# Turned query features for more row pairs, with their key sums weighed by GpSimd: a linear-attention and gMLP kernel on one Trainium2 core

## The chip, the cores and the metric

The kernel runs on one core of one Trainium2 chip. The metric is the device time of one execution in microseconds (us). Several executions are timed and the median is taken; one further execution is recorded by the hardware profiler.

The engines are called by their short names: PE (TensorE, matrix products and transposes by a matmul with the identity), DVE (VectorE), ACT (ScalarE), POOL (GpSimd), SP (SyncE, which here only issues DMA transfers). Each has an instruction queue of its own and works through it in order.

## The reference

Two blocks read the same `x` of 2048 rows and 512 columns, in float32, and their results are added to it: `x + A(layernorm(x)) + B(layernorm(x))`.

```python
# A: linear attention, 32 heads of 16, Hedgehog features (32 per head)
pq = einsum("bhsd,hdf->bhsf", q, w_phi); pk = the same of k
phi_q = concat([softmax(pq), softmax(-pq)]); phi_k = the same of pk
kv  = einsum("bhsf,bhsd->bhfd", phi_k, v)
z   = einsum("bhsf->bhf", phi_k)                    # key sums
num = einsum("bhqf,bhfd->bhqd", phi_q, kv)
den = einsum("bhqf,bhf->bhq", phi_q, z) + 1e-6
o   = num / den;  A = o @ wo
# B: gMLP with 688 gated columns
u, v = split(gelu(xn @ w_in));  v = layernorm(v)
v = w_sp @ v + b_sp;            B = (u * v) @ w_out
```

## The kernel before, in words

The 2048 rows are 16 row tiles of 128 (`NT`), taken as 8 pairs. A tile's query features are 1024 values a row (`NF`). Products in float32 are made of three matmuls of high and low parts (`mm3`, lines L56 to L58).

The work goes through four stages. To about 205 us: projections, key features, `kv` and the key sums. The softmax exponentials of the queries (`e`) go to a DRAM tensor `e_d`. To about 290 us: the inputs of the gate. To 489 us: the spatial product with `w_sp` (tile name `g`), in 32 chunks, four for each pair of row blocks. After a pair's last chunk, `gate` multiplies by `u` and turns the result on DVE in blocks of 32x32, and DMAs store it to `u_d` and `ur_d` in a layout from which it can be loaded already transposed. From 489 us on, the last stage goes over the pairs; this is the loop `for i in range(0, NT, 2)` of the kernel. For each pair PE does: the projection of the gated values of tile i (`project_u`, `pout<-wu,...`), the attention of the pair (`attend`, `po<-f,kvT`), `project_u` of tile i+1, and the output projection of both tiles (`project_o`), whose result is added to `out` in DRAM by an accumulating DMA from POOL's queue (`out<-xr`, L1022).

`attend` needs the features transposed: features on the partitions. There are two ways to that.

- *Transposed on PE.* `attend_T` makes sixteen transposes for a pair (`ptq`, L972 or L974), and ACT copies the results out of PSUM (`f<-ptq`, L976).
- *Turned.* `turn_q` turns the tile on DVE in 32x32 blocks (STREAM_TRANSPOSE `qtmp<-et`, L559), four DMAs store it to the DRAM tensor `q_d` (L562), and one loads it transposed (`f<-q_d`, L564). PE has nothing to do. Tiles from `TQ` = 10 on (pairs 5 to 7) go this way.

Ahead of either, `q_fin` finishes a tile's features, all on DVE: the product of the exponentials with the key sums `zb` (L545, `qtmp<-et,zb`), a sum over each half head (L546), four small steps that make the factor `w` (L547 to L550), and the product of the exponentials with it (L552). `load_q` loads a tile's exponentials from `e_d` to a tile `et` by SP's queue. Tiles 4 to 9 are then copied from `et` into a buffer of the pair, `er`, by a DMA of POOL's queue (L940), from which PE transposes them; tiles 2 and 3 are transposed from `et` itself; tiles 0 and 1 have been finished much earlier and are loaded as `eq` by `first_q`.

`ahead(i)` runs after a tile's output projection and does the work for later ones: `features(i+3)`, the load of the exponentials of tile i+5, and of the gated values of tile i+4. The order of instructions on each engine comes from a scheduler, which follows the order of the code and the points set by `tc.issue_after`. `GATE_LAST` names the iteration in which the last pair's gate is made.

Of the kernel before, what the change touches and what calls it, by code (L numbers as in the profile page):

```python
# [10 lines left out]
F32 = mybir.dt.float32  # L11
F32R = mybir.dt.float32r
AF = mybir.ActivationFunctionType
ALU = mybir.AluOpType
# [26 lines left out]
def mixer(ctx: ExitStack, tc: tile.TileContext, x, x_t, wv, wqkT, phi_bd, wo, w_in, wst, b_r, w_out, out):  # L41
    nc = tc.nc
    pe, act, dve, pool, sp = nc.tensor, nc.scalar, nc.vector, nc.gpsimd, nc.sync
# [27 lines left out]
    def xz_tile(n, dt, name):  # L71
        return xz.tile([P, SL], dt, tag="xz", name=name)[:, :n]
# [3 lines left out]
    e_d = dram.tile([NT, P, NF + 2 * H], F32, name="e_d")  # L76
# [5 lines left out]
    q_d = dram.tile([NT, P, NF], F32, name="q_d")  # L82
# [16 lines left out]
    def heads(ap):  # L99
        return ap.rearrange("p (h d) -> p h d", d=DH)  # L100
# [76 lines left out]
    with ExitStack() as p0:  # L177
        res = p0.enter_context(left("p0res", 1))
        wk = p0.enter_context(left("p0wk", 2))
# [253 lines left out]
        p = ps.tile([P, D], F32, tag="mm", name="proj")  # L433
# [7 lines left out]
        p = ps.tile([P, D], F32, tag="mm", name="proj")  # L441
# [18 lines left out]
        p = ps.tile([P, D], F32, tag="mm", name="proj")  # L460
# [77 lines left out]
        sp.dma_start(et[:, :NF + 2 * H], e_d[s])  # L538
        return et

    def q_fin(et, tmp, zb):

        e, r, t, w = et[:, :NF], *(et[:, NF + k * 2 * H:NF + (k + 1) * 2 * H] for k in range(3))
        den = et[:, NF + 6 * H:QW]
        dve.tensor_tensor(tmp, e, zb, op=ALU.mult)  # L545
# [6 lines left out]
        return e, dve.tensor_tensor(heads(e), heads(e), bc(w, 2 * H), op=ALU.mult).ins  # L552

    TQ = 10

    def turn_q(s, dst, e, f, eng):

        NC8 = NF // P
        dve.transpose(dst.rearrange("p (m c t) -> p m c t", c=NC8, t=BL), e.rearrange("p (c m j) -> p m c j", c=NC8, j=BL))  # L559
        w = NC8 * BL  # L560
        for b in range(P // BL):
            eng.dma_start(q_d[s, :, b * w:(b + 1) * w].rearrange("(m j) w -> j m w", j=BL),  # L562
                          dst[b * BL:(b + 1) * BL].rearrange("p (m w) -> p m w", w=w))
        eng.dma_start(f[:, s % 2], q_d[s])  # L564

    QC = 4
    NQ = NT // QC
# [151 lines left out]
    for s in range(NT):  # L719
        p = zproj((kv_ps_p, zc, zbp, za)[s % 4], s, w2, (0, 1) if s % 2 == 0 else (1, 0))  # L720
# [7 lines left out]
        for k, q in p:  # L728
            ins = act.activation(z[:, k], q, AF.Gelu_apprx_tanh, scale=r_x[:, s:s + 1]).ins
# [30 lines left out]
    gt = mid.enter_context(right("gt", 1))  # L760
# [64 lines left out]
    def slot(name, dt=F32):  # L825
        return xz_tile(2 * FH, dt, name)
# [27 lines left out]

    lasts, wu = [None] * 9, []

    def first_q(s):
        e = slot("eq", F32R)[:, :NF]
        sp.dma_start(e.bitcast(F32), e_d[s, :, :NF])
        return e  # L860
# [11 lines left out]
    g, es, ets, ft, ep = {}, {}, {}, {}, {}  # L872
    for n in range(NC):
        i = SEQ[n][0]
        if n % NQ == 1 and i < NP - 1:
            z = load_z1(i)
        products(n, g)
        if n % NQ == NQ - 1 and i < NP - 1:
            c = gt.tile([P, 2, FU], F32, tag="c", name="c")
            cq = c[:, :, :FH].rearrange("p k (j f) -> p k j f", j=2)  # L880
            cb = drain(i, g, cq)
            g = {}
        if n + 3 < NC:
            raw[n + 3] = load_a(n + 3)
        if n + 2 < NC:
            A[n + 2] = prep_a(n + 2, raw.pop(n + 2))
        if n % NQ == NQ - 1 and i < NP - 1:
            turn = gate(i, cb, z, c, z, prep_a.last)
            if i < NP - 2:
                turn()  # L890
        if n == NC - 4:
            stage_w()
        if n == NC - 3:
            zs = slot("zb", F32R)
            zb, ident_r = zs[:, :NF].bitcast(F32), zs[:, NF:NF + P]
            round_h(act, ident_r, ident)
            sp.dma_start(zb, zb_d)
            uT = [first_gate(0)]
            ets[2] = load_q(2, slot("et"))
            es[2], last = q_fin(ets.pop(2), slot("qtmp")[:, :NF], zb)  # L900
        if n == NC - 2:
            es[0], es[1] = first_q(0), first_q(1)
            t = xz_tile((KF + 1) * P, F32R, "u1")
            us = {1: load_u(1, t[:, :KF * P].bitcast(F32), t[:2 * REM, KF * P:(KF + 1) * P])}
    cb = drain(NP - 1, g, slot("c").rearrange("p (k j f) -> p k j f", k=2, j=2))
# [6 lines left out]
    gt = p2.enter_context(right("gl", 1))  # L912
    cw = ctx.enter_context(left("cw", 1))
    wk = ctx.enter_context(left("cwk", 2))
    fin = []

    def fetch_u(i):
        return load_u(i, cw.tile([P, KF * P], F32, tag="u", bufs=4, name="u"),
                      cw.tile([2 * REM, P], F32R, tag="rt", bufs=6, name="rt"))

    def er_pair(name):
        return cw.tile([P, 2, NF], F32R, tag="er", bufs=3, name=name)

    def features(s):
        with tc.issue_after(fin[-1]):
            tmp = slot("qtmp")[:, :NF]
            es[s], ins = q_fin(ets.pop(s), tmp, zb)
        fin.append(ins)
        if s == 3:
            return  # L930
        if s >= TQ:
            if s % 2 == 0:
                ft[s] = er_pair("f").bitcast(F32)
            turn_q(s, tmp, es.pop(s), ft[s - s % 2], pool)
            return
        e = es[s]
        if s % 2 == 0:
            ep[s] = er_pair("er")
        es[s] = ep[s - s % 2][:, s % 2]
        lasts[6] = pool.dma_start(es[s].bitcast(F32), e).ins  # L940
# [18 lines left out]

    def attend_T(s):  # L960

        if s in ft:
            t = ft[s].rearrange("p k (b c t) -> p (k b) c t", c=NF // P, t=BL)
            return [t[:, :, 2 * g:2 * g + 2].rearrange("p b c t -> p c b t") for g in range(NG)]
        fs = []
        for g in range(NG):
            pt = pst.tile([P, 2, 2, P], F32, tag="tr", name="ptq")
            for a in range(2):
                for k in range(2):
                    src = group(es[s + k], 2 * g + a)  # L970
                    if src.dtype == F32:
                        pe.transpose(pt[:, a, k], src, ident)  # L972
                    else:
                        pe.transpose(pt[:, a, k].bitcast(F32R), src, ident_r)  # L974
            f = wk.tile([P, 2, 2 * P], F32, tag="f", bufs=NG + 1, name="f")
            lasts[5] = act.activation(f, pt.rearrange("p a k b -> p a (k b)"), AF.Copy).ins  # L976
            fs.append(f)
        return fs
# [47 lines left out]
                dve.tensor_tensor(xr[:, cs], q, xr[:, cs], op=ALU.add)  # L1026
                sp.dma_start(out[rows, cs], xr[:, cs])

    GATE_LAST = 8

    fT = attend_T(0)
    wk.tile([P, D], F32, tag="xr", bufs=3, name="xr")
    wk.tile([P, 10 * QP], F32, tag="gap", name="gap")
    wk.tile([P, NG, 2 * P], F32R, tag="oTh", name="oT")
    with tc.issue_after(lasts[5]), tc.issue_after(lasts[1]), tc.issue_after(fin[-1]):
        for c in range(ND):
            rows = [(m * QP, (m + 1) * QP) for m in range(c // 2 * 8 + c % 2, (c // 2 + 1) * 8, 2)]
            load_w(wo, rows, wo_h[:, c], wo_l[:, c], cw.tile([P, D], F32, tag="wof", bufs=4, name="wof"))
# [5 lines left out]

    def ahead(i):

        if 3 < i + 3 < NT:
            features(i + 3)
        if i + 5 < NT:
            ets[i + 5] = load_q(i + 5, slot("et"))  # L1050
        if i + 4 < NT:
            us[i + 4] = fetch_u(i + 4)

    p, nxt = {}, dict(enumerate(uT))
    for i in range(0, NT, 2):
# [60 lines left out]
```

## Time and profile before

| what | us |
|---|---|
| median of 3 runs | 618.63 (618.36 to 619.22) |
| the profiled execution's own time | 618.89 |
| its span, first to last instruction | 617.0 |
| PE busy | 610.3 (99%) |
| DVE busy | 517.6 (84%) |
| ACT busy | 269.6 (44%) |
| POOL busy | 128.8 (21%) |

The span starts with the first instruction and ends with the last; the execution's own time has 1.9 us more around it. Busy shares are means over stages of different kinds. In the last stage, the place of this change, what counts is the order in which things come due there: PE is dense, and the rows that follow in the prediction tell what comes just in time for it. In profile rows "idle before <-" names what ended an engine's wait, and a transfer's time is given from its issue to its landing.

### The profile page before, as it was taken

The page shows a single profiled execution, that of the slowest core. Times are in us where ns is not written, and L with a number is a line of the kernel's source. Part 1 is how long each engine was busy: PE and PEld are TensorE (multiplying, and loading weights), DVE is VectorE, ACT ScalarE, POOL GpSimd, SP SyncE. Part 2 cuts the span into 40 slices and gives each one's busy share as a digit, 9 for nine tenths or more (in the row PEclk, how much of TensorE's full clock was granted, in tenths as well). Part 3 has the DMA queues.
Part 4 walks back from the last instruction along what each step waited for, and adds up shares of the span by engine and source line. Part 5 has one row for each costly group of instructions (what it writes and reads, how often), then busy time and mean ns, then how long its engine had stood idle before and what let it go on. Part 6 is the DMA issues. An engine that isn't in the chain of part 4 may idle for free.

```text
span 617.0 us, 11407 instructions
## 1 busy us (share of the span) xinstructions
PE 610.3 (99%) x4318; PEld 557.1 (90%) x4318; DVE 517.6 (84%) x925; ACT 269.6 (44%) x424; POOL 128.8 (21%) x226
## 2 busy tenths in 40 slices
PE   8999999999999999999999999999999999999997
PEld 6888888888889999999999999999999987777775
DVE  5999999999978498989899898797979889999711
ACT  5653334323523467876444444344436343333221
POOL 4123232232110015442000000000000132234330
PEclk9999999999999999999999999999999999999999
DMA  8557876666446768001463744636355798987873
GB/s 308 196 136 168 227 176 173 156 163 171 125 141 163 263 218 289 2 1 35 149 144 122 198 101 148 155 95 186 97 164 181 222 364 287 303 239 210 221 161 65
DMA packets 55534, 106.81 MB, mean 173 GB/s; under 512 B 12136, under 2 KB 22248, under 8 KB 55240
## 3 DMA queue, kind: packets, MB, share of 16 engines
q1 hardware_dynamic: 40424, 60.77, 32.4%
q0 software_dynamic: 12752, 39.69, 25.2%
q10 hardware_dynamic: 2304, 5.64, 2.4%
q8 instruction: 34, 0.56, 0.4%
q14 instruction: 20, 0.16, 0.1%
HBM read 64.76 MB, written 33.71 MB: 160 GB/s over the span
## 4 chain that ended last, share of the span: by engine, by line
PE 95%; DMA 3%; DVE 0%; SPq 0%; ACT 0%; issue 0%; DVEq 0%; ACTq 0%
PE g L58 11%; PE g L57 11%; PE g L56 11%; PE proj L57 7%; PE proj L56 7%; PE proj L58 7%; PE zps L56 6%; PE zps L57 6%; PE zps L58 6%; PE pout L56 6%; PE pout L58 5%; PE pout L57 5%; PE po L989 1%; PE kvps L355 1%; PE pout L1003 1%; DMA wst__2228<-in_w_in 1%
## 5 line engine op out<-in xcount | busy, mean ns | idle before, releaser
L57 PE MATMUL g<-B,A 128*128 128x344 f32 x448 | 143.4, 320 | 0.0
L56 PE MATMUL g<-B,A 128*128 128x344 f32 x448 | 142.9, 319 | 0.0
L58 PE MATMUL g<-B,A 128*128 128x344 f32 x448 | 140.4, 321 | 0.1
L56 PEld LDWEIGHTS g<-B,A 128*128 128x128 f32 x448 | 84.3, 188 | 0.0
L57 PEld LDWEIGHTS g<-B,A 128*128 128x128 f32 x448 | 84.2, 188 | 0.0
L58 PEld LDWEIGHTS g<-B,A 128*128 128x128 f32 x448 | 83.6, 188 | 0.4 <-DVE A L52 0.4
L48 ACT ACTIVATE A<-S 128x512 fp32r<-128x512 f32 x64 | 40.1, 629 | 59.4 <-PE g L58 28.4
L52 DVE TENSOR_TENSOR A<-S,A 128x512 fp32r<-128x512 f32 x64 | 43.7, 686 | 11.2 <-ACT A L48 11.0
L48 ACT ACTIVATE A<-wf 128x512 fp32r<-128x512 f32 (+1 forms) x64 | 33.4, 523 | 44.5 <-PE g L58 28.1
L56 PE MATMUL proj<-wqk_h,xT 128*128 128x512 f32 x128 | 50.1, 391 | 0.0
L58 PE MATMUL proj<-wqk_h,xT 128*128 128x512 f32 x128 | 49.8, 389 | 0.0
L57 PE MATMUL proj<-wqk_l,xT 128*128 128x512 f32 x128 | 49.8, 389 | 0.0
L123 ACT ACTIVATE e<-e,r_x 128x1024 f32<-128x1024 f32 x26 | 29.7, 1148 | 42.3 <-DVE e L122 41.3
L768 POOL DMA_DIRECT2D z1t<-z_d x16 | 8.7, 546 | 162.5 <-DMA wf<-in_wst 127.2
L56 PE MATMUL zps<-w_0h,xT 128*128 128x344 f32 x128 | 41.0, 320 | 0.1
L57 PE MATMUL zps<-w_1l,xT 128*128 128x344 f32 x128 | 40.8, 319 | 0.0
L57 PE MATMUL zps<-w_0l,xT 128*128 128x344 f32 x128 | 40.8, 319 | 0.0
L58 PE MATMUL zps<-w_0h,xT 128*128 128x344 f32 x128 | 40.8, 319 | 0.0
L56 PE MATMUL zps<-w_1h,xT 128*128 128x344 f32 x128 | 40.7, 318 | 0.0
L58 PE MATMUL zps<-w_1h,xT 128*128 128x344 f32 x128 | 40.6, 319 | 0.0
L52 DVE TENSOR_TENSOR A<-wf,A 128x512 fp32r<-128x512 f32 (+1 forms) x64 | 35.3, 555 | 3.5 <-ACT A L48 3.3
L126 DVE TENSOR_REDUCE sm<-e 128x64 f32<-128x1024 f32 x26 | 31.1, 1201 | 2.5 <-ACT e L123 2.4
(224 smaller groups left out, 1435.9 us busy)
## 6 DMA issues: line engine op xcount, KB each, us to landing
wf<-in_wst SPq DMA_DIRECT2D x64, 256.0 KB, 3.2
e_d<-e POOLq DMA_DIRECT2D x16, 544.0 KB, 4.6
et<-e_d SPq DMA_DIRECT2D x16, 544.0 KB, 6.3
z_d<-z1f ACTq DMA_DIRECT2D x16, 344.0 KB, 2.9
z1t<-z_d POOLq DMA_DIRECT2D x16, 344.0 KB, 4.5
zacc<-e POOLq DMA_DIRECT2D x10, 512.0 KB, 4.9
u<-u_d SPq DMA_DIRECT2D x15, 320.0 KB, 5.9
xt<-in_x SPq DMA_DIRECT2D x16, 256.0 KB, 3.7
```

The lines of the kernel that those rows point to most:

```text
L48: return act.activation(h, src, AF.Copy).ins
L52: return (eng or dve).tensor_tensor(l, src, h.bitcast(F32), op=ALU.subtract).ins
L56: pe.matmul(dst, ah, bh, start=start, stop=False)
L57: pe.matmul(dst, ah, bl, start=False, stop=False)
L58: return pe.matmul(dst, al, bh, start=False, stop=stop).ins
L123: softmax_pair.last = less, act.activation(e, e, AF.Exp, scale=scale).ins
L126: dve.tensor_reduce(sm, heads(e), axis=AX.X, op=ALU.add)
L355: i = pe.matmul(kv_acc[k:k + QP, m // 4], vs[:, m * QP:(m + 1) * QP], e[:, m * HP:(m + 1) * HP], start=first and m < 4 and len(ready) == n ...
L768: pool.dma_start(t[:, k, :FH], z1_d[2 * i + k])
L989: lasts[3] = pe.matmul(po[r][c * QP:(c + 1) * QP, k], kvT[rows, m // 2, cols], fs[m // 4][rows, m // 2 % 2], start=True, stop=True).ins
L1003: lasts[2] = pe.matmul(p, rt, w, start=False, stop=i == NT - 1 and k == 1).ins
```

## The change

It has six parts.

1. `TQ` goes from 10 to 6: tiles 6 to 9 (pairs 3 and 4) are turned instead of transposed on PE.
2. Pair 0 is turned too, already in the stage before: after the gates of i = 2 and i = 4, tile 0's and tile 1's features are loaded from `e_d`, turned by DVE and stored to `q_d`. Four loads `f<-q_d` of 256 KB take the place of the two loads of `eq`.
3. For tiles 4 to 15 the product with the key sums is made by POOL, in a new function `weigh`, called from `ahead`. `q_fin` leaves it out there.
4. The stores to `q_d` and the loads of `f` go by SP's queue instead of POOL's (those of pair 0's early turn are stored by POOL's).
5. `GATE_LAST` goes from 8 to 6, one pair sooner.
6. The point after which the output weights are loaded is another (`lasts[0]` for `lasts[5]`), since pair 0 has no copies `f` any more.

Pairs 1 and 2 are still transposed on PE, and only tiles 4 and 5 still have an `er` copy.

```diff
-    def q_fin(et, tmp, zb):
+    def q_fin(et, tmp, zb, weighed=False):
...
-        dve.tensor_tensor(tmp, e, zb, op=ALU.mult)
+        if not weighed:
+            dve.tensor_tensor(tmp, e, zb, op=ALU.mult)
...
-    TQ = 10
+    TQ = 6
...
-        eng.dma_start(f[:, s % 2], q_d[s])
...
+            if i in (2, 4):
+                s = i // 2 - 1
+                e, t = (gt.tile([P, 2, FU], F32, tag=tag, name=name).rearrange("p k f -> p (k f)")[:, :NF]
+                        for tag, name in (("c", "c"), ("z1", "z1t")))
+                pool.dma_start(e, e_d[s, :, :NF])
+                turn_q(s, t, e, pool)
...
-            es[0], es[1] = first_q(0), first_q(1)
+            fq = [slot("f")[:, :NF].rearrange("p (k b c t) -> p k b c t", k=2, c=NB // 2, t=BL) for h in range(2)]
+            for k in range(2):
+                for h in range(2):
+                    sp.dma_start(fq[h][:, k], q_d[k].rearrange("p (b h w) -> h p b w", h=2, w=QB // 2)[h])
...
+    def weigh(s):
+        weighed[s] = slot("qtmp")[:, :NF]
+        pool.tensor_tensor(weighed[s], ets[s][:, :NF], zb, op=ALU.mult)
...
-            tmp = slot("qtmp")[:, :NF]
-            es[s], ins = q_fin(ets.pop(s), tmp, zb)
+            tmp = weighed.pop(s, None)
+            if s > 3:
+                es[s], ins = q_fin(ets.pop(s), tmp, zb, True)
+            else:
+                tmp = slot("qtmp")[:, :NF]
+                es[s], ins = q_fin(ets.pop(s), tmp, zb)
...
-            turn_q(s, tmp, es.pop(s), ft[s - s % 2], pool)
+            turn_q(s, tmp, es.pop(s), sp)
...
-    GATE_LAST = 8
+    GATE_LAST = 6
...
-    with tc.issue_after(lasts[5]), tc.issue_after(lasts[1]), tc.issue_after(fin[-1]):
+    with tc.issue_after(lasts[0]), tc.issue_after(lasts[1]), tc.issue_after(fin[-1]):
...
+        if i + 4 < NT:
+            weigh(i + 4)
         if 3 < i + 3 < NT:
             features(i + 3)
...
+        if TQ <= i + 3 < NT:
+            sp.dma_start(ft[(i + 3) // 2 * 2][:, (i + 3) % 2], q_d[i + 3])
```

The order on POOL at the beginning of the last stage, before the change. The last gate's stores (`u_d`, `ur_d`) come first, then the outputs of pair 0 and the copies of tiles 4, 5 and 6; `z1t` is the load for the last gate.

```order
L820 DMA ur_d<-z1t 32x6x32 x4
L1022 DMA out<-xr 128x512 x2
L940 DMA er<-et 128x1024 x3
L768 DMA z1t<-z_d 128x688 x2
L1022 DMA out<-xr 128x512 x2
L940 DMA er<-et 128x1024 x2
```

The same place after it. The products `qtmp<-et,zb` are those of tiles 4, 5, 6, then of 7 and 8, then of 9; the first `er` copy is that of tile 4, the second that of tile 5.

```order
L821 DMA ur_d<-z1t 32x6x32 x4
L933 TENSOR_TENSOR qtmp<-et,zb 128x1024 x3
L1040 DMA out<-xr 128x512 x2
L955 DMA er<-et 128x1024
L933 TENSOR_TENSOR qtmp<-et,zb 128x1024 x2
L955 DMA er<-et 128x1024
L769 DMA z1t<-z_d 128x688 x2
L933 TENSOR_TENSOR qtmp<-et,zb 128x1024
L1040 DMA out<-xr 128x512 x2
```

Where the copies of tiles 4 and 5 followed the first two outputs directly, three products now stand ahead of the outputs and two more between the two copies.

On SP, in pair 1 and after, the order before had only loads (exponentials `et`, gated values `u` and their remainder `rt`):

```order
L538 DMA et<-e_d 128x1088
L836 DMA u<-u_d 128x640
L837 DMA rt<-ur_d 96x128
L836 DMA u<-u_d 128x640
L538 DMA et<-e_d 128x1088 x2
```

After it, the stores of tile 6 and 7, which wait for DVE's turn, and their loads stand between them:

```order
L538 DMA et<-e_d 128x1088
L837 DMA u<-u_d 128x640
L838 DMA rt<-ur_d 96x128
L837 DMA u<-u_d 128x640
L564 DMA q_d<-qtmp 32x4x256 x4
L538 DMA et<-e_d 128x1088
L1075 DMA f<-q_d 128x1024
L564 DMA q_d<-qtmp 32x4x256 x4
```

A tile's load `f` follows its own stores, one load of exponentials later.

More of the change, by code (lines that the diff above doesn't have):

```diff
@@ L552, in q_fin, with turn_q @@
         return e, dve.tensor_tensor(heads(e), heads(e), bc(w, 2 * H), op=ALU.mult).ins
-    TQ = 10
[L556 to L560, printed above, removed]
+    TQ = 6
+    NB = NF // P
+    QB = NB * BL
+    def turn_q(s, dst, e, eng):
+        dve.transpose(dst.rearrange("p (m c t) -> p m c t", c=NB, t=BL), e.rearrange("p (c m j) -> p m c j", c=NB, j=BL))
         for b in range(P // BL):
-            eng.dma_start(q_d[s, :, b * w:(b + 1) * w].rearrange("(m j) w -> j m w", j=BL),
-                          dst[b * BL:(b + 1) * BL].rearrange("p (m w) -> p m w", w=w))
-        eng.dma_start(f[:, s % 2], q_d[s])
+            eng.dma_start(q_d[s, :, b * QB:(b + 1) * QB].rearrange("(m j) w -> j m w", j=BL),
+                          dst[b * BL:(b + 1) * BL].rearrange("p (m w) -> p m w", w=QB))
     QC = 4
@@ L855, in mixer @@
     lasts, wu = [None] * 9, []
[L857 to L860, printed above, removed]
     def stage_w():
@@ L922, in er_pair @@
         return cw.tile([P, 2, NF], F32R, tag="er", bufs=3, name=name)
+    weighed = {}
+    def weigh(s):
+        weighed[s] = slot("qtmp")[:, :NF]
+        pool.tensor_tensor(weighed[s], ets[s][:, :NF], zb, op=ALU.mult)
     def features(s):
         with tc.issue_after(fin[-1]):
-            tmp = slot("qtmp")[:, :NF]
-            es[s], ins = q_fin(ets.pop(s), tmp, zb)
+            tmp = weighed.pop(s, None)
[4 more added lines that the diff above has]
+                es[s], ins = q_fin(ets.pop(s), tmp, zb)
         fin.append(ins)
@@ L960, in attend_T @@
     def attend_T(s):
+        if not s:
+            t = [f.rearrange("p k b c t -> p (k b) c t") for f in fq]
+            return [t[g // 2][:, :, g % 2 * 2:g % 2 * 2 + 2].rearrange("p b c t -> p c b t") for g in range(NG)]
         if s in ft:
@@ L1027, in project_o @@
                 sp.dma_start(out[rows, cs], xr[:, cs])
-    GATE_LAST = 8
+    GATE_LAST = 6
     fT = attend_T(0)
+    wk.tile([P, 2, 2 * P], F32, tag="f", bufs=NG + 1, name="f")
     wk.tile([P, D], F32, tag="xr", bufs=3, name="xr")
```

## The prediction, made before the changed kernel was run

> **What bounds the kernel now.** I read the page's busy times first, then the stretches of 20 us in the last stage, then the chain of waits there, and last the single transfers and GpSimd instructions that the change moves.
>
> ```profile
> PE 610.3 (99%) x4318; PEld 557.1 (90%) x4318; DVE 517.6 (84%) x925; ACT 269.6 (44%) x424; POOL 128.8 (21%) x226
> L58 PE MATMUL g<-B,A 128*128 128x344 f32 x448 | 140.4, 321 | 0.1
> ```
>
> ```profile
> 300.00:400.00 100.00, 100.00 (x636) 100.00 (x636) 86.67 (x183) 42.22 (x71) 4.25 (x8) 1.00 0.52 140
> 500.00:520.00 20.00, 20.00 (x125) 16.08 (x124) 19.35 (x32) 6.24 (x12) 2.94 (x4) 1.00 0.92 302
> 520.00:540.00 20.00, 20.00 (x135) 16.23 (x134) 19.35 (x32) 8.61 (x16) 6.83 (x10) 1.00 1.01 318
> 540.00:560.00 20.00, 20.00 (x152) 15.39 (x151) 19.44 (x27) 6.97 (x13) 7.47 (x12) 1.00 0.90 254
> 580.00:600.00 20.00, 20.00 (x116) 15.90 (x115) 5.35 (x6) 4.95 (x8) 6.99 (x10) 1.00 0.67 175
> ```
>
> The columns of the second fence are the stretch, its length, the busy time of PE, PE's weight loads, DVE, ACT and POOL, then granted clock, DMA share and GB/s. PE is the bound: it never pauses in these stretches, and its clock is full. But three others are near their limit behind it from 500 to 560 us: DVE is busy 19.4 of 20 us and the DMA engines 0.90 to 1.01 of the time, while POOL has 12 to 17 us free. So a matmul taken away shortens the end one for one, as long as nothing that PE needs comes later than PE does.
>
> ```profile
> 489.13 1.33 PE ptq L974 x16
> 494.43 1.02 PE po L989 x32
> 505.04 1.75 PE ptq L972 x16
> 510.67 1.02 PE po L989 x32
> 521.28 1.31 PE ptq L974 x16
> 526.57 1.02 PE po L989 x32
> 537.18 1.34 PE ptq L974 x16
> 542.48 1.02 PE po L989 x32
> 553.09 1.31 PE ptq L974 x16
> 558.38 1.02 PE po L989 x32
> 572.86 1.02 PE po L989 x32
> ```
>
> These are rows of the chain (start, length, what): the sixteen transposes of pairs 0 to 4, and the attention matmuls of pairs 0 to 5. Pairs 5 to 7, whose features are already turned, have no transposes.
>
> **What goes from PE.** Pairs 0, 3 and 4 lose 1.33, 1.34 and 1.31 us, in sum 3.98 us. The period from one pair's attention to the next tells the same: 15.90 us (526.57 to 542.48) with transposes, 14.48 (558.38 to 572.86) without, 1.42 for each pair; I take the rows' own 3.98. ACT loses 12 copies that followed them, and was 44% busy: nothing.
>
> **What the new POOL instruction costs.** Twelve key-sum products of 128x1024 move from DVE to POOL. The trace has no two-input POOL instruction of that size. Its nearest rows:
>
> ```profile
> L169 POOL TENSOR_TENSOR mask<-mask 128x128 f32<-128x128 f32 x1 | 0.5, 454 | 0.1
> L175 POOL MEMSET zacc<- 128x1024 f32 x1 | 0.9, 942 | 0.0
> L171 POOL MEMSET mask<- 128x128 f32 x1 | 0.2, 194 | 0.0
> L270 POOL TENSOR_SCALAR nm<-mv_x 128x1 f32<-128x1 f32 x5 | 1.2, 239 | 24.0 <-DVE mv_x L266 19.4 <-DVE mask L312 4.6
> ```
>
> The memset grows by 748 ns over 896 elements, so its fixed part is 0.09 us; the one-element operation shows 0.24. With 0.09 fixed, the 454 ns product costs 2.8 ns an element and 3.0 us at 1024; with 0.24 it costs 1.7 ns and 2.0 us. I take 2.4, between the two. The lowest bound is the memset of the same size, 0.94, which reads nothing; no gain below that is possible, since the product must write as much. The Trainium skill ("GPSIMD Engine Reference", section 3.1) has a measured fp32 tensor_tensor of 2048 elements at 4497 ns on GpSimd; half of it, 2.25 us, is an estimate from that page, and would put my sum 0.45 us lower. No run here shows it.
>
> **Where POOL's time lies on the path.** Pair 2 still has transposes, at 521.28 us, and they read the two row tiles that POOL copies by its `er` DMAs. POOL runs in order. Before, those copies stood behind the first two output transfers only; now five products stand ahead of the second copy.
>
> ```profile
> 500.27 0.34 SPq L538 DMA_DIRECT2D et<-e_d  x1
> 502.74 0.32 SPq L538 DMA_DIRECT2D et<-e_d  x1
> et<-e_d SPq DMA_DIRECT2D x16, 544.0 KB, 6.3
> 503.71 0.96 POOL L1022 DMA_DIRECT2D out<-xr  x1 [7.26 <-ACT xr L1021]
> 505.98 0.88 POOL L1022 DMA_DIRECT2D out<-xr  x1 [1.31 <-ACT xr L1021]
> 508.82 0.56 POOL L940 DMA_DIRECT2D er<-et  x1 [1.96 <-DVE et L552]
> 513.95 0.55 POOL L940 DMA_DIRECT2D er<-et  x1 [4.58 <-DVE et L552]
> DMA to landing us min/median/max: 4.3/5.1/5.9
> ```
>
> The last row is the answer for those two `er` transfers alone. Step by step: tile 5's features arrive by 500.27 + 6.3 = 506.6, its product ends at 509.0. Tile 6's, issued at 502.74, land at 509.0; that product ends at 511.4. Two output issues (0.96 and 0.88) bring POOL to 513.3, the copy of tile 4 (0.56) to 513.8, the products of tiles 7 and 8 (4.8) to 518.6 (tile 8's load follows pair 1's transposes, at 505.5 now, and lands by 511.8, in time). Only then is tile 5's copy issued, 4.6 us later than 513.95, and it lands 5.1 us on, at 523.7. PE, 1.33 us ahead after pair 0, wants it at 521.28 - 1.33 = 519.95. So PE stalls 3.75 us ahead of pair 2. With the product at 2.0 us the stall is 2.55, at 3.0 it is 5.55, at 0.94 it is nothing (landing 519.3); the transfer's 4.3 to 5.9 moves it by 0.8 either way.
>
> **DVE.** It loses twelve products and gains four turns in this stage:
>
> ```profile
> L545 DVE TENSOR_TENSOR qtmp<-et,zb 128x1024 f32<-128x1024 f32 x16 | 19.5, 1219 | 0.5 <-DMA et<-e_d 0.5
> L559 DVE STREAM_TRANSPOSE qtmp<-et 128x1024 f32<-128x1024 f32 x6 | 7.4, 1239 | 0.0
> L552 DVE TENSOR_TENSOR et<-et 128x1024 f32<-128x1024 f32 x16 | 19.6, 1224 | 0.4
> L52 DVE TENSOR_TENSOR ul<-u,uh 128x640 fp32r<-128x640 f32 x15 | 12.2, 815 | 7.4 <-ACT uh L48 7.4
> ```
>
> That is 12 x 1.22 less 4 x 1.24, 9.7 us off an engine beside the path: nothing by itself, but it pays for waiting on POOL. In its queue DVE now waits for each product, and pair 1's rounding rests stand behind the wait for tile 6 (to 511.4): they are then done by about 515, where they ran at 514.70 before, so 0 to 0.5 us, inside the stall that follows.
>
> **Pairs 3 and 4.** A turned tile needs a DVE turn, four stores and a load back. Before the change, the first such tile (10) took from 542.47 (turn) to 558.0 (its load landed):
>
> ```profile
> 542.47 1.24 DVE L559 STREAM_TRANSPOSE qtmp<-et 128x1024 f32<-128x1024 f32 x1
> 551.20 0.56 POOL L564 DMA_DIRECT2D f<-q_d  x1 [4.11 <-DMA q_d<-qtmp]
> DMA to landing us min/median/max: 6.8/6.8/6.8
> ```
>
> Tile 7's product ends at 516.2, its turn can stand near 523, and 15.5 us on is 538.5; its attention is due at 542.48 - 2.67 + 3.75 = 543.6. Pair 4 has more. Nothing, then, with 0 to 3 us as the bound if DMAs are late. SP takes 50 more issues of 0.3 us and POOL sheds them; SP's own loads are issued pairs ahead.
>
> **The rest.** The last gate a pair sooner moves 4.1 us of DVE work, and the order of the output weights' loading has no price in the trace: nothing, for DVE's 9.7. The two early turns run in a stage with DVE 87% busy and DMAs half free. DVE may stand there until the stores of the gate before have landed (0 to 3 us each). The weight chunks are prepared two ahead, 42 matmuls a chunk at 636 in 100 us, so 6.6 us each: nothing, upper end 2.
>
> **Sum.** 618.89 (the profiled run; span 617.0) - 3.98 + 3.75 = 618.66. That run stands 0.26 above the median of 618.63, so 618.4 against the median. About 0.2%, 1.2 us, is what a measurement of this kernel can tell from no change: 617.4 to 619.9 counts as the same.
>
> **Rivals.** *The product is short (faster).* Each 0.1 us off it takes 0.3 off the stall. From 2.07 us down the change is faster; at 1.9 the time is 616.9, at 1.2 or less all 3.98 us stay, 614.7. For it: the memset's 0.94 and the low end 2.0. Against: the 454 ns for only 128 elements.
>
> *POOL and DVE hold each other up (slower).*
>
> ```profile
> 227.22 1.31 POOL L739 TENSOR_SCALAR nb<-mv,rstd 128x1 f32<-128x1 f32 x1
> 227.25 1.23 DVE L552 TENSOR_TENSOR et<-et 128x1024 f32<-128x1024 f32 x1
> 232.99 0.26 POOL L739 TENSOR_SCALAR nb<-mv,rstd 128x1 f32<-128x1 f32 x1
> ```
>
> A one-element POOL instruction takes 0.26 us alone and 1.31 beside a 1.23 us DVE product of two SBUF operands: it waits that product out. If the products of tiles 6, 7 and 8 each wait out one such DVE instruction (0.82 to 1.22), the copy lands 2.5 to 3.7 us later and the time is 620.9 to 622.1. It decides from 1.5 us of such waiting in all. The Trainium skill ("SBUF — State Buffer", section "Who interferes with whom") says that such a DVE instruction and a GpSimd one that reads SBUF exclude each other for a whole instruction, in both directions; the rows agree for POOL as the loser, and no row shows DVE as the loser. If DVE loses, tile 3's last product (502.25 before) may wait for tile 4's on POOL; a stall of PE there gives the late copy time and is not added.
>
> *DMAs become the bound (slower).* Four `er` copies of 0.5 MB give way to four stores and four loads: 2 MB more, at some 300 GB/s 6.6 us of traffic into stretches already at 0.90 to 1.01. If a third of it reaches pair 2 or 3, the time is 620.6. Against: the share falls to 0.67 by 580, and loads run pairs ahead.
>
> *The early turns stall the product stage (slower).* Two stalls of over 0.75 us each end above 619.9.
>
> **Chances.** Late copy as summed 0.34 (0.27 of it within the same; alone 617.0 to 620.4); short product 0.33; mutual waiting 0.20; DMAs 0.09; early turns 0.04. Faster is 0.33 and 0.03 of the first, 0.36; same 0.27 and 0.02 of the DMAs, 0.29; slower the rest, 0.35. The range goes from 614.4, just under the full gain, to 622.4, just over the mutual waiting.
>
> **What would show it.** Right: no `ptq` for pairs 0, 3, 4; products on POOL of 2.0 to 3.0 us; PE idle 2.5 to 5.5 us ahead of pair 2's transposes and put down to the `er` transfer, and nowhere else. Wrong: products of about 1.2 us, or the copy landing before 520; products of widely differing lengths, or DVE instructions of two operands beyond 1.3 us, for mutual waiting; PE idle ahead of an attention of pairs 3 to 7 for DMAs; idle before 489 us for the early turns.

## The result, and the profile after

The changed kernel takes 635.92 us (median of 4 runs, 635.01 to 637.11) against 618.76 for the kernel before: 1.027 times as long, 95% interval 1.025 to 1.028. The forecast was 618.4, with a range to 622.4. The profiled execution took 637.11 us, its span is 635.4.

First the page's busy times, then the stretches of the last stage (same columns as before: stretch, length, busy PE, weight loads, DVE, ACT, POOL, granted clock, DMA share, GB/s).

```profile
PE 613.8 (97%) x4270; PEld 556.9 (88%) x4270; DVE 524.4 (83%) x919; ACT 260.0 (41%) x412; POOL 145.0 (23%) x214
```

```profile
490.00:510.00 20.00, 16.59 (x107) 13.10 (x107) 17.11 (x24) 6.62 (x13) 9.34 (x10) 1.00 0.86 289
510.00:530.00 20.00, 16.11 (x81) 11.96 (x81) 19.62 (x22) 3.62 (x7) 14.79 (x11) 0.76 0.76 219
530.00:550.00 20.00, 20.00 (x125) 15.99 (x124) 19.62 (x26) 6.92 (x12) 6.62 (x5) 0.99 0.85 230
550.00:570.00 20.00, 16.60 (x87) 12.44 (x87) 19.76 (x30) 4.90 (x7) 6.47 (x4) 0.83 0.99 284
610.00:636.00 26.00, 17.45 (x115) 14.07 (x113) 2.83 (x5) 2.88 (x5) 2.59 (x3) 0.94 0.38 71
```

PE has 48 instructions less and is busy 3.5 us more: the transposes are gone, but the matmuls run slower in two stretches, where the granted clock is 0.76 and 0.83. And PE pauses there, which it did not do before in this stage. PE's rows of the changed kernel, around its three pauses (start, length, instruction, and in brackets the idle time with what ended it):

```profile
493.88 0.45 PE L1007 MATMUL po<-f,kvT 64*32 64x256 f32 x8
...
504.40 0.60 PE L990 MATMUL ptq<-ident,et 128*128 128x128 f32 x4
508.41 1.53 PE L990 MATMUL ptq<-ident,et 128*128 128x128 f32 x12 [3.41 <-DVE et L553]
...
511.02 0.63 PE L56 MATMUL pout<-wu,uh 128*128 128x512 f32 x1
511.45 0.63 PE L57 MATMUL pout<-wu,uh 128*128 128x512 f32 x1
...
513.89 0.40 PE L58 MATMUL pout<-wu,ul 128*128 128x512 f32 x1
514.12 0.39 PE L56 MATMUL pout<-wu,uh 128*128 128x512 f32 x1
...
515.36 0.88 PE L1007 MATMUL po<-f,kvT 64*32 64x256 f32 x24
...
525.37 0.80 PE L58 MATMUL pout<-woh,oT 128*128 128x512 f32 x1 [3.88 <-DVE oT L52]
...
537.72 0.66 PE L1007 MATMUL po<-f,kvT 64*32 64x256 f32 x15
...
552.19 1.09 PE L1007 MATMUL po<-f,kvT 64*32 64x256 f32 x32
...
561.71 0.80 PE L58 MATMUL pout<-woh,oT 128*128 128x512 f32 x1 [3.40 <-DVE oT L52]
...
573.21 1.09 PE L1007 MATMUL po<-f,kvT 64*32 64x256 f32 x32
```

The first pause is in the middle of pair 1's transposes (tile 3's features are late); the other two are in the output projections of pairs 1 and 3 (DVE's rounding rest `oT` is late). After a pause matmuls start 0.43 us apart (511.02, 511.45) instead of 0.23 (513.89, 514.12), for some 5 us.

From attention to attention the time divides without a rest. Pair 0 begins 0.48 us sooner than before (493.88 against 494.36 in the same rows of before). The way to pair 1 is 21.48 us, 5.24 longer: 3.41 of pause, and the other 1.83 I put down to the slow matmuls behind it. To pair 2 it is 22.36, 6.46 longer: 3.88 and 2.58 in the same way. To pair 3, 14.47, 1.43 shorter, the transposes' gain. To pair 4, 21.02 where 15.90 stood: the gain of 1.43, then 3.40 of pause and 3.15 of slow clock. The last three pairs are as before. After the last attention 3.5 us more go, all of them behind PE's last matmul, in an instruction that the prediction did not speak of. It is POOL's final drain (columns: count, then shortest, median and longest in ns), before and after:

```profile
L1112 POOLq DRAIN  x3: 40/102/4902, 611.4 to 616.8; - x3
```

```profile
L1135 POOLq DRAIN  x3: 40/93/8342, 626.3 to 635.1; - x3
```

The sum: -0.48 + 5.24 + 6.46 - 1.43 + 5.12 + 3.5 = 18.4, the difference of the spans (635.4 and 617.0).

What made DVE late? Its rows in the changed kernel, first single instructions (start, length), then groups (count, busy us, mean ns, idle before):

```profile
501.98 1.21 DVE L547 TENSOR_REDUCE et<-qtmp 128x64 f32<-128x1024 f32 x1
...
503.84 2.38 DVE L548 TENSOR_TENSOR et<-et 128x64 f32<-128x64 f32 x1
...
507.13 1.22 DVE L553 TENSOR_TENSOR et<-et 128x1024 f32<-128x1024 f32 x1
...
509.52 1.15 DVE L548 TENSOR_TENSOR et<-et 128x64 f32<-128x64 f32 x1
510.71 2.26 DVE L549 SCALAR_TENSOR_TENSOR et<-et 128x32 f32<-128x32 f32 x1
...
516.03 4.55 DVE L548 TENSOR_TENSOR et<-et 128x64 f32<-128x64 f32 x1
...
547.62 2.62 DVE L52 TENSOR_TENSOR ul<-u,uh 128x640 fp32r<-128x640 f32 x1
...
555.84 1.33 DVE L548 TENSOR_TENSOR et<-et 128x64 f32<-128x64 f32 x1
```

```profile
L548 DVE TENSOR_TENSOR et<-et 128x64 f32<-128x64 f32 x16 | 14.3, 891 | 0.1
...
L549 DVE SCALAR_TENSOR_TENSOR et<-et 128x32 f32<-128x32 f32 x16 | 6.6, 414 | 0.3
...
L52 DVE TENSOR_TENSOR ul<-u,uh 128x640 fp32r<-128x640 f32 x15 | 15.0, 1003 | 14.0 <-ACT uh L48 14.0
```

Its small instructions of two SBUF operands, 219 ns in the mean before, take up to 4.55 us. They end when POOL's products end:

```profile
503.70 2.44 POOL L933 TENSOR_TENSOR qtmp<-et,zb 128x1024 f32<-128x1024 f32 x1 [5.82 <-PE pout L58]
...
507.68 5.23 POOL L933 TENSOR_TENSOR qtmp<-et,zb 128x1024 f32<-128x1024 f32 x2 [1.54 <-DMA et<-e_d]
...
515.74 4.75 POOL L933 TENSOR_TENSOR qtmp<-et,zb 128x1024 f32<-128x1024 f32 x2
...
523.02 0.59 POOL L955 DMA_DIRECT2D er<-et  x1 [2.53 <-DVE et L553]
```

```profile
L933 POOL TENSOR_TENSOR qtmp<-et,zb 128x1024 f32<-128x1024 f32 x12 | 30.2, 2522 | 36.7 <-DMA et<-e_d 28.6 <-PE pout L58 5.8 <-DMA er<-et 2.2
```

The instruction at 516.03 stood through two products in a row, until 520.6. POOL's products vary little (2.52 us in the mean, 2.4 to 3.1): DVE is the loser. Over the stage the three groups took 17.2 us more than before (14.3 for 3.5, 6.6 for 3.0, 15.0 for 12.2).

The holding is enough for the second pause (4.3 us held, 3.88 of pause) and for a part of the two others. Tile 3's last product starts at 507.13, where it was 502.25 before: 2.2 us of that were held, and 2.7 had been lost ahead of it, since the reduction at 501.98 ran at 499.25 before. In that time DVE waited 1.40 us for the output weights and 1.32 us for gated values. Ahead of the third pause 2.9 us were held (547.62 and 555.84); DVE also makes two turns of 1.23 us there, and never idles.

### The profile page after: what moved, and what is told of

The parts are those of the page before. It is cut to its first block, busy times and chain, and to the rows that moved or that the text cites. A ratio compares the mean times of both kernels' runs of the same rounds, so it can differ in the third digit from the quotient of the medians.

```text
span 635.4 us, 11400 instructions
## 1 busy us (share of the span) xinstructions
PE 613.8 (97%) x4270; PEld 556.9 (88%) x4270; DVE 524.4 (83%) x919; ACT 260.0 (41%) x412; POOL 145.0 (23%) x214
## 4 chain that ended last, share of the span: by engine, by line
PE 82%; DVE 7%; DMA 6%; issue 2%; SPq 2%; ACT 0%; DVEq 0%; ACTq 0%
PE g L58 11%; PE g L57 11%; PE g L56 11%; PE proj L56 7%; PE proj L58 7%; PE proj L57 7%; PE zps L58 6%; PE zps L56 6%; PE zps L57 6%; PE pout L58 3%; PE pout L56 3%; PE pout L57 3%; DMA u<-u_d 2%; DMA zacc<-e 1%; PE kvps L355 1%
## 5 line engine op out<-in xcount | busy, mean ns | idle before, releaser
L933 POOL TENSOR_TENSOR qtmp<-et,zb 128x1024 f32<-128x1024 f32 x12 | 30.2, 2522 | 36.7 <-DMA et<-e_d 28.6
```

Of the source, the lines that this page charges most:

```text
L933: pool.tensor_tensor(weighed[s], ets[s][:, :NF], zb, op=ALU.mult)
```

## The experiments

All but the first are timed beside the kernel before on the same chip, where that took 619.2 to 619.5 us. In the kernels with fills, and in those without a product anywhere, the key sums are missing from the denominators of tiles 4 to 15. Where the table says "no product on POOL", and for pair 0, pairs 0 and 4 and "three pairs", DVE makes the product. Four names for causes: L, POOL's products and DVE exclude each other; Q, SP's queue holds up loads behind the transfers of turned features; D, DVE has no room; G, the sooner last gate.

| kernel | median us | ratio (95%) | PE pauses over 1 us in its profile | POOL's drain |
|---|---|---|---|---|
| the change | 635.9 | 1.025 to 1.028 | 3.4, 3.9, 3.4 | 8.3 |
| no product on POOL | 637.7 | 1.027 to 1.032 | 1.5, 2.4, 10.4, 1.2 | 8.5 |
| product on POOL alone | 638.7 | 1.030 to 1.035 | 8.8, 1.1, 4.3 | 4.9 |
| fills for products | 628.1 | 1.012 to 1.022 | 1.3, 2.9, 2.4 | 8.3 |
| pair 0 alone, SP's queue | 622.0 | 1.003 to 1.007 | none | 8.8 |
| pair 0 alone, POOL's queue | 618.8 | 0.998 to 1.000 | none (0.65) | 5.4 |
| three pairs, POOL's queue | 635.0 | 1.023 to 1.028 | 6.8, 7.0 | 6.2 |
| no product on POOL, gate late | 636.5 | 1.024 to 1.030 | 1.2, 3.9, 7.8 | 8.2 |
| pairs 0 and 4, POOL's queue | 621.6 | 1.002 to 1.005 | 1.4, 2.0, 1.5 | 5.8 |
| no product anywhere | 630.8 | 1.016 to 1.024 | 1.8, 4.1 | 8.2 |
| SP's queue alone | 624.1 | 1.006 to 1.012 | 1.0 | 8.3 |
| pair 0, its loads on POOL | 622.9 | 1.004 to 1.007 | 1.6 | 6.3 |
| no product, POOL's queue | 628.6 | 1.011 to 1.016 | 8.1 | 6.3 |
| no product, POOL's queue, gate late | 620.1 | 0.999 to 1.003 | 1.2 | 6.0 |
| no product, SP's queue, gate late | 631.9 | 1.016 to 1.023 | 2.4, 3.8, 2.3 | 8.6 |
| fills, POOL's queue, gate late | 632.4 | 1.019 to 1.023 | 3.6, 1.7, 4.9 | 6.0 |
| product, POOL's queue, gate late | 641.7 | 1.034 to 1.037 | 2.7, 3.9, 1.3, 9.4, 1.5 | 6.1 |

**The product back on DVE.**

```diff
-        if i + 4 < NT:
-            weigh(i + 4)
...
-            if s > 3:
-                es[s], ins = q_fin(ets.pop(s), tmp, zb, True)
+            es[s], ins = q_fin(ets.pop(s), tmp, zb)
```

> The changed kernel with the product of exponentials and key sums back on DVE for all tiles; pair 0 and pairs 3 and 4 stay turned, stores and loads of turned features stay on SP. Theory L (POOL's products and DVE's two-operand instructions hold each other up, and that makes the stalls ahead of pair 1's transposes, in pair 1's and pair 3's output projection): no DVE instruction of this stage beyond 1.3 us, the three PE gaps of 3.4, 3.9 and 3.4 us gone or under 1 us, time 615 to 620. Rival Q (SP's longer queue, with four loads for pair 0 and the stores of turned tiles ahead of the next exponentials, makes things late): the gaps stay, time 628 or more.

637.7 us. DVE's instructions are back to 0.23 us and the three pauses are gone, as L has it, but others came, up to 10.4 us, ahead of the attention of pairs 3, 4, 5 and 7: turned features arrive late. L alone is not the cause.

**The product on POOL as the only change.**

```diff
+        if i + 4 < NT:
+            weigh(i + 4)
...
+                es[s], ins = q_fin(ets.pop(s), tmp, zb, True)
```

> The kernel before with one part of the change alone: POOL makes the product with the key sums for tiles 4 to 15. Pairs 0, 3 and 4 are still transposed on PE, turned features go by POOL's queue as before. Theory L: the same stretched DVE instructions and gaps of several us, time 626 to 638 (the change's 636 with 4 us of transposes more and fewer turns on DVE). Rival Q: DVE is relieved and nothing is late, 617 to 621.

638.7 us, just above L's range. The edit is against the kernel before. This part alone costs 19 us, with DVE instructions of up to 4.5 us and a pause of 8.8 us in pair 1.

**Fills in place of POOL's products.**

```diff
-        weighed[s] = slot("qtmp")[:, :NF]
-        pool.tensor_tensor(weighed[s], ets[s][:, :NF], zb, op=ALU.mult)
+        t = slot("qtmp")
+        pool.tensor_tensor(t[:, :1], ets[s][:, :1], zb[:, :1], op=ALU.mult)
+        for _ in range(2):
+            pool.memset(t, 1.0)
+        weighed[s] = t[:, :NF]
```

> The changed kernel, but POOL's product is replaced by a one-element product that waits for the same load, and two fills of 1376 elements that write the same buffer and read nothing (by the fill of 1024 at 0.94 us some 1.25 us each, 2.7 us in all against 2.5 for the product). The key sums are left out of the attention's denominators. POOL's time, queue and the waits of DVE for it are the same, only POOL does not read SBUF for long. Theory L: DVE's small instructions return to 0.2 to 0.35 us, time 616 to 624. Rival W (DVE waits too long for POOL's results in its queue, whatever POOL does): time 630 or more.

628.1 us (625.8 to 632.4), 7.9 below the change and 4 above what L expected. POOL is occupied as long, and DVE's first small step is never held:

```profile
L935 POOL MEMSET qtmp<- 128x1376 f32 x24 | 30.7, 1279 | 1.2
```

```profile
L548 DVE TENSOR_TENSOR et<-et x16: 181/183/225, 222.0 to 572.2; 128x64 f32<-128x64 f32 x16
```

So the holding does not come from POOL's being busy; what the long fills leave out is the reading of SBUF. The Trainium skill ("SBUF — State Buffer", section "Who interferes with whom") says this: a DVE instruction of two SBUF inputs contends with a GpSimd instruction that reads SBUF, "not with one that only writes it", and the later one blocks for the whole instruction. The traces agree, with 0.18 to 0.23 us for that step beside fills and up to 2.38 beside one product. The 4.55 us, through two products in a row, are more than that section states. The other 8.7 us over the kernel before stay without it.

**Pair 0 alone, on SP's queue and on POOL's.** The first is the product back on DVE and `TQ` at 10; the second also moves the transfers to POOL (and takes SP's loads from `ahead`):

```diff
-    TQ = 6
+    TQ = 10
...
-            turn_q(s, tmp, es.pop(s), sp)
+            turn_q(s, tmp, es.pop(s), pool)
+            pool.dma_start(ft[s - s % 2][:, s % 2], q_d[s])
```

> The changed kernel with DVE's own product, and only pair 0 turned early; pairs 3 and 4 are transposed on PE again (turned from tile 10 on), stores and loads of turned features on SP. Theory L: no gap, 618.8 less 1.3 for pair 0's transposes, 616.8 to 618.3. Rival Q: a gap ahead of pair 1's transposes of about 1 us or more, since the four loads for pair 0 delay the exponentials and gated values behind them on SP: 618 to 622.

> Pair 0 turned early as in the change, DVE's own product, pairs 3 and 4 transposed on PE, and the stores and loads of turned features on POOL's queue, as before the change. Against the run with the same on SP's queue (622.0, of which POOL's last drain took 8.8 us where the kernel before has 4.9). Theory S (the long drain comes with taking these transfers off POOL's queue): drain back at 4.9 us, time 617.5 to 618.8, the first gain over the kernel before. Rival E (it comes with the early turn's transfers on POOL): drain 8.3 or more, time 621 to 623.

622.0 and 618.8 us. The first has neither L's gain nor Q's pause. Between them the drain changes most, 8.8 against 5.4 us:

```profile
L1129 POOLq DRAIN  x3: 40/93/8762, 610.9 to 620.1; - x3
```

```profile
L1128 POOLq DRAIN  x3: 40/93/5397, 611.7 to 617.6; - x3
```

Pair 0's own gain is 0.65 us of 619.45, not told apart from none by its interval. In the second trace 1.09 of the 1.33 us arrive at pair 0's attention; 0.89 are lost on the way to pair 1, 0.65 of it in a pause in that pair's transposes, 0.54 on the way to pair 3, and the drain is 0.5 longer.

**SP's queue as the only change.**

```diff
-            turn_q(s, tmp, es.pop(s), ft[s - s % 2], pool)
+            turn_q(s, tmp, es.pop(s), ft[s - s % 2], sp)
...
+        if TQ <= i + 3 < NT:
+            sp.dma_start(ft[(i + 3) // 2 * 2][:, (i + 3) % 2], q_d[i + 3])
```

> The kernel before with one part of the change alone: the stores and loads of turned features (tiles 10 to 15) go by SP's queue. Theory S (POOL's last drain is longer without them on its queue): PE's end as before, drain 8 us or more instead of 4.9, time 621.5 to 623.5. Rival: drain as before, the move costs nothing, 618.5 to 620.5.

624.1 us: 4.9 more, 3.4 of it in the drain (8.3 against 4.9) and 1.0 in a pause ahead of the last pair. (The profiled execution took 625.3; 2.0 us of its length were lost ahead of this stage, where the edit changes nothing.) Eight kernels with these transfers on SP drain for 8.2 to 8.8 us, and those with them on POOL for 4.9 to 6.3.

**Three pairs turned, product on DVE, POOL's queue; and the last gate late, on SP's.**

```diff
-    GATE_LAST = 6
+    GATE_LAST = 8
```

> Pairs 0, 3 and 4 turned, DVE's own product, last gate at pair 3, and the stores and loads of turned features on POOL's queue. Against the run with the same on SP's queue (637.7; PE gaps ahead of the attention of pairs 3, 4, 5 and 7 of 1.5, 2.4, 10.4 and 1.2 us). Theory Q (SP's queue: tile 11 was turned by 565.5, but its stores were issued at 573 behind waiting loads): the 10.4 us gap falls to 4 or less, time 622 to 629. Rival D (DVE is full and turns late whatever queue follows): gaps of the same size, 632 to 638.

> As the run without POOL's product (637.7, turned features on SP's queue), but with the last gate at its old place, one pair later. Theory D (DVE's load ahead of pair 5): 4.1 us of gate work leave the stretch ahead of pair 5 and its stores leave SP's queue there; the 10.4 us gap falls by 4 to 8 us, time 629 to 634, with a new gap of a few us ahead of pair 6 or 7. Rival: the gate's place doesn't matter, 636 to 639.

635.0 and 636.5 us. With these products on DVE the queue is worth 2.6 us, 2.3 of it drain, as D has it. The gate's place is worth 1.2, less than D had: the pause ahead of pair 5 went, and one of 7.8 us came ahead of pair 6. In the first:

```profile
520.00:540.00 20.00, 20.00 (x126) 16.04 (x125) 19.55 (x29) 6.47 (x12) 7.70 (x12) 1.00 0.93 270
```

```profile
547.37 1.96 PE L1004 MATMUL po<-f,kvT 64*32 64x256 f32 x32 [6.84 <-issue]
```

DVE is full until PE waits for pair 3's turned features, 6.8 us. The sum, from DVE's rows of before: a tile follows the last after 4.8 us of features, 0.7 of `ul` and 0.6 of `oT`, 6.1 us; a turn adds 1.15. A pair takes DVE 12.2 us untransposed by it and 14.5 turned; PE takes 15.9 and 14.5. By this sum it was the transposes on PE that let DVE get ahead. (Taking the product off DVE too, below, is worth 4.6 to 6.9 us in three pairs of kernels.)

**Pairs 0 and 4, POOL's queue, gate late.**

```diff
-    TQ = 6
+    TQ = 8
...
-    GATE_LAST = 6
+    GATE_LAST = 8
```

> Pairs 0 and 4 turned, DVE's own product, last gate at its old place, turned features on POOL's queue. DVE has 2.5 us more than before instead of 5. If two tiles more fit into DVE's time: 616 to 617.5, no gap over 0.5 us. If DVE is already too full: gaps ahead of pairs 4 to 6, 619 to 625.

621.6 us: two tiles more already don't fit, with pauses of 2.0 and 1.5 us ahead of pairs 4 and 6, and one of 1.4 in pair 1's transposes.

**Pair 0's loads on POOL.**

```diff
-                    sp.dma_start(fq[h][:, k], q_d[k].rearrange("p (b h w) -> h p b w", h=2, w=QB // 2)[h])
+                    pool.dma_start(fq[h][:, k], q_d[k].rearrange("p (b h w) -> h p b w", h=2, w=QB // 2)[h])
```

> Pair 0 turned early, all else as before except the last gate at pair 3, and the four loads of pair 0's turned features on POOL's queue, which is idle there, instead of SP's. If the gap of 0.65 us ahead of pair 1's transposes and the longer first period (17.1 us against 16.2) came from SP's longer queue: gap gone, time 617.5 to 618.5, faster than before by 0.2 % or so. If the loads crowd the DMA engines whatever queue issues them: same as with SP's queue, 618.5 to 619.5.

622.9 us: missed both ways. The pause ahead of pair 1 grew from 0.65 to 1.6 us and the drain from 5.4 to 6.3. Why those loads are worse there was not followed.

**No product anywhere.** DVE sums the exponentials themselves:

```diff
-        dve.tensor_reduce(t, heads(tmp), axis=AX.X, op=ALU.add)
+        dve.tensor_reduce(t, heads(e if weighed else tmp), axis=AX.X, op=ALU.add)
```

> The changed kernel without the product with the key sums on any engine from tile 4 on: the sums are taken of the exponentials themselves, so the key sums are missing from the denominators of those tiles. Turns, queues and the last gate are those of the change. Against the run with DVE's own product (637.7, gaps up to 10.4 us) and the run with fills on POOL (628.1). Theory D (DVE is full: with the product a turned pair takes it 14.5 us, as long as PE): 12 x 1.14 us off DVE close the gaps, PE gaps under 1 us each, time 616 to 620 with the long drain. Rival Q (SP's queue): gaps of 3 us or more stay, 624 or more.

> As the run without any product, but with the stores and loads of turned features on POOL's queue: what turning three pairs could give if DVE had the room. The key sums are missing from the denominators from tile 4 on. Theory: three pairs' transposes less (4 us), drain about 5 to 6 us: 614.5 to 617. Rival Q' (POOL's queue delays the copies of tiles 4 and 5 or the outputs): gaps of 2 us or more, 618 or more.

630.8 and 628.6 us, both well above what was expected if DVE's room were all. With the product's time taken off DVE and POOL a pause of 4.1 us is left on SP's queue and one of 8.1 on POOL's. The second one shows why. SP, DVE and PE rows:

```profile
555.66 4.89 SPq L819 DMA_DIRECT2D u_d<-zt  x4
560.73 1.22 SPq L538 DMA_DIRECT2D et<-e_d  x1
...
570.61 1.22 DVE L547 TENSOR_REDUCE et<-et 128x64 f32<-128x1024 f32 x1 [8.18 <-DMA et<-e_d]
...
572.48 0.80 PE L58 MATMUL pout<-woh,oT 128*128 128x512 f32 x1 [8.05 <-DVE oT L52]
```

The sooner gate's stores stand ahead of a load of exponentials on SP; DVE waits 8.2 us for that load; `oT`, which PE wants, stands behind it on DVE.

**The same with the gate late, on POOL's queue and on SP's.** The edit is `GATE_LAST` at 8, as above.

> No product on any engine from tile 4 on (the key sums are missing from those denominators), turned features on POOL's queue, and the last gate at its old place. Against the run with the gate at pair 3 (628.6, one gap of 8.1 us, where DVE waited 8.2 us for a load of exponentials that SP issued behind the gate's stores). Theory G (the sooner gate puts its stores ahead of the last loads of exponentials on SP): that gap gone, time 614.5 to 617.5. Rival M (DMA engines too full for the loads whatever the order): a gap of 3 us or more ahead of pairs 3 to 5, 621 or more.

> The same with turned features on SP's queue, as in the change. Against the run with the gate at pair 3 (630.8, gaps of 1.8 and 4.1 us where DVE waited for exponentials). Theory Q (SP's waits for the turn hold up the loads behind them): gaps of 1.5 to 4 us in pairs 2 to 4 stay, 623 to 630. If the gate's stores alone were it: no gap over 0.5 us, 617.5 to 619.5 with the long drain.

620.1 and 631.9 us, both above their ranges. On POOL's queue the gate's place was the whole pause of 8.1 us (628.6 to 620.1, G), and one of 1.2 in pair 1's transposes is left; on SP's queue nothing was won. There DVE waits for exponentials five times; the first:

```profile
519.70 2.17 SPq L564 DMA_DIRECT2D q_d<-qtmp  x4
521.91 1.59 SPq L538 DMA_DIRECT2D et<-e_d  x1
526.45 0.34 SPq L1069 DMA_DIRECT2D f<-q_d  x1
526.89 1.99 SPq L564 DMA_DIRECT2D q_d<-qtmp  x4
...
530.49 1.22 DVE L547 TENSOR_REDUCE et<-et 128x64 f32<-128x1024 f32 x1 [4.07 <-DMA et<-e_d]
...
534.36 0.50 PE L58 MATMUL pout<-woh,oT 128*128 128x512 f32 x1 [2.39 <-DVE oT L52]
```

The load is issued behind four stores and has landed 8.6 us later, where 6.3 was the median before. What SP itself waits for, from 505 to 570 us (total us, times, longest):

```profile
SPq L1069 <- DMA q_d<-qtmp: 17.5, 8, 5.3
SPq L564 <- DVE et L549: 1.5, 2, 1.1
SPq L564 <- DVE et L553: 0.8, 2, 0.5
```

The stores wait for DVE for 2.3 us in all. The loads `f` (L1069) wait 17.5 us for the stores to land, and all that comes after stands behind them: the stores at 526.89 are those of a turn that DVE had finished at 524.1. In the changed kernel it is the same, 13.6 us at `f` and 0.8 at the stores. Q's effect is shown: 11.8 us between two kernels that differ in that queue alone, 2.6 of it drain, and DVE's waits of over 1 us for exponentials add up to 13.3 us against 2.8. How much of that is late issue and how much slower landing (median 7.0 us against 5.8) is not separated. In the other four pairs of kernels that differ in this queue it is worth 2.2 to 4.9 us, 1.9 to 3.4 of it drain. And the first of the two is the most that turning three pairs gave in any run: 620.1, no gain, even with products that cost nothing. PE does end 1.3 us sooner there (611.25 in the trace against 612.55); the drain, 1.1 us longer, takes most of that back.

**Fills and products with the gate late, on POOL's queue.** The edits are those of the fills, of the queue and of `GATE_LAST` above; the second keeps the product.

> The change with the fills in place of POOL's product (they read nothing; the key sums are missing from the denominators), turned features on POOL's queue, last gate at its old place. Against the run with fills, SP's queue and the sooner gate (628.1). If lock, queue and gate are all there is: the late copy of tile 5 costs 1 to 2 us, else no gap, 616 to 620. If POOL's queue is too full with fills and turned features together: gaps of 3 us or more, 622 or more.

> The change with POOL's product as it is, but turned features on POOL's queue and the last gate at its old place. Theory L (product and DVE hold each other up): DVE instructions of up to 4.5 us and gaps of 3 to 4 us ahead of pair 1's transposes and in pair 1's output projection as in the change, third gap smaller, 625 to 634; 6 us or more above the run with fills. If queue and gate were the most of it: under 622.

632.4 and 641.7 us: 9.3 us apart, L once more, though the second is 7.7 above L's range. The fills' kernel takes 12.3 us more than the one without them, and its three pauses stand ahead of what reads transfers of POOL's (`er`, then twice turned features): POOL's queue now has the fills' time and turned features. The second kernel, which has the change's products, is 5.8 us slower than the change: beside the products, SP's queue and the sooner gate did help, in sum. The first pause of the fills is the one that the prediction had summed:

```profile
517.76 0.65 POOL L933 TENSOR_TENSOR qtmp<-et,zb 128x1 f32<-128x1 f32 x1
518.35 0.60 POOL L959 DMA_DIRECT2D er<-et  x1
...
524.39 1.89 PE L996 MATMUL ptq<-zb,er 128*128 128x128 f32 x13 [3.56 <-DMA er<-et]
```

## Why the prediction was wrong, point by point

**PE's transposes**: right. The period to pair 3 is 1.43 us shorter (1.42 foreseen); of pair 0's 1.33 only 0.48 arrived at its attention.

**The product's time**: right. 2.52 us measured, 2.4 taken from two rows of other sizes.

**The late copy of tile 5**: not the cause here. It was issued at 523.0 (518.6 foreseen), since POOL, through with its products at 520.5, waited 2.5 us for DVE's held features; and it cost nothing, since PE came to pair 2's transposes only at 532.3. Where DVE was not held, the mechanism showed: with fills the copy was issued at 518.35 and PE paused 3.56 us, 3.75 foreseen. With fills on the change's own queues it was 1.27 us, so the closeness of 3.56 is in part luck.

**DVE**: the step that failed. "9.7 us off an engine beside the path: nothing by itself, but it pays for waiting on POOL" counted DVE's instructions at their old lengths. They were held for 17.2 us by POOL. The rival of mutual waiting was there, and it even said where DVE may lose first, at tile 3; but its price took only POOL as the loser, 2.5 to 3.7 us, it put a stall there at nothing because it "gives the late copy time", it did not follow DVE's delay to `oT`, and it got a chance of 0.20. The run with the product alone costs 19 us; fills in the product's place are 7.9 and 9.3 us faster than products. That no row of before showed DVE as the loser says little, since the kernel before has no POOL product of that length beside DVE.

**SP's queue**: "SP's own loads are issued pairs ahead" was wrong. Those loads stand in order behind stores, and behind loads `f` that wait for the stores to land; DVE waits for them, and `oT` stands behind that. It is 11.8 us in the pair of kernels without products and with the late gate, 2.2 to 4.9 in the four others.

**The last gate**: put at nothing because of DVE's 9.7 us; its stores, which move ahead of loads on SP, were not followed. 8.5 us in the kernels without products on POOL's queue; on SP's queue 1.2 with DVE's product and nothing without.

**What a pause costs**: taken as its own length. The change's three pauses cost 1.8 to 3.2 us more each, by the slow matmuls that follow.

**The end**: POOL's drain was no part of the sum. 3.4 us.

The parts don't add up to 17: each was to pay for another (the product on POOL for the turns on DVE, SP's queue for POOL's time), and they were measured in kernels that differ in the others. How the 17 us of the change itself divide among them stays open, but for L's 7.9 and the drain's 3.4.

## What to carry to other kernels

Before work is taken off a full bound engine and given to the next, sum that next engine's time for one period against the bound's new period; here 14.5 us met 14.5, and the lead that hid everything else was gone. When a moved instruction reads the same memory as another engine, price both as the loser, for the whole length of the longer one, or of several in a row. Follow in each in-order queue what stands behind a new wait: a load back that waits for its stores to land holds what is behind it, and a late load holds the small instruction on which the bound engine waits.

## What the runs showed of the hardware

- A DVE instruction of 128x64 with two SBUF operands took 4.55 us beside two POOL products in a row; it did not get its turn between them. DVE's turns and reductions, with one operand, kept their lengths.
- Every pause of PE of 3.4 us or more in these traces (3.4 to 10.4) is followed by 3 to 6 us of matmuls at 0.43 us instead of 0.23. After a pause of 2.39 us they were 0.23 apart from the second on; pauses in between cost sometimes 0.1 and sometimes 1.8 us more. One pause of only 1.80 us (no product anywhere, SP's queue, 533.4) was followed by 3 us at 0.43 too, from the fifth matmul on. The Trainium skill ("TensorE: Matmul & The Clock Gate", Part 1) puts the limit for idle gaps at about 3.4 us, and the cold and warm pitch of 512 columns at 426.7 and 215.7 ns; the traces agree in the cold pitch, and have 0.23 for the warm one; for the limit, the pause of 1.80 us does not agree.
- POOL's final drain takes 4.9 us in the kernel before, 5.4 to 6.3 in those with early turns and turned features on POOL's queue, 8.2 to 8.8 with turned features on SP's. What it waits for is open: in the changed kernel the last output had landed by 631.0, and the drain ended at 634.6.
